# Sliding dilated attention with a gated FFN on one core: V kept twice in lines of positions, and a tile's eight copies of V loaded in two pieces

## The chip, the cores and the metric

The kernel runs on one core of one Trainium2 chip. The metric is the device time of one execution in microseconds; the time before is 239.39 us, the median of three runs (238.27 to 239.54). Names of engines in the profile: PE is TensorE's matmuls and PEld its weight loads, DVE is VectorE, ACT is ScalarE, POOL is GpSimd and SP is SyncE.

## The reference

A transformer block on 2048 positions of width 512, in bf16. Six vectors of modulation come from a small matrix product with a conditioning vector. The attention has 32 heads of 16 columns; each position looks at itself and at seven earlier positions, two apart.

```python
h = _layernorm(x) * (1 + ca) + sa
qkv = h @ wqkv                          # 32 heads of 16
idx = pos[:, None] - 2 * arange(8)      # the eight positions looked at
logits = einsum('bhsd,bhswd->bhsw', q, k[idx]) * scale    # -1e9 where idx < 0
attn = softmax(logits)
o = einsum('bhsw,bhswd->bhsd', attn, v[idx])
x = x + ga * (o @ wo)
h = _layernorm(x) * (1 + cb) + sb
x = x + gb * ((silu(h @ w1) * (h @ w3)) @ w2)             # inner width 1792
```

## The kernel before

**Tiles.** The 2048 positions are 16 tiles of 128. The first normalization and the projections of Q, K and V go by five groups of tiles: 0 and 1, 2 and 3, 4 to 7, 8 to 11, 12 to 15 (`LN1`). The normalized rows of a group are turned by TensorE (`tr`, groups 0 to 2) or by DMA transposes (groups 3 and 4, that is tiles 8 to 15); ScalarE or VectorE scales the turned rows with the modulation (L621, L644, L651), and TensorE makes Q, K (L691) and V (L711) of them. The attention goes by pairs of tiles, the FFN by six groups.

**Logits.** Q and K lie with the columns of the heads on the partitions, so that one VectorE multiplication per tile (L742, 128 x 4096) makes the products of all eight offsets: K is just read 2 w positions further back. TensorE sums over the 16 columns of a head, 32 positions at a time in four parts of the array (L752). VectorE takes maximum, difference, sum and reciprocal, ScalarE the exponential, and VectorE scales a pair's weights (L797, one operation for both tiles).

**Values.** For V the positions must be shifted across partitions. So ScalarE copies a tile of V from the PSUM into one of three buffers (L721), a DMA stores it in an HBM scratch with one row per position, after 16 rows of zeros, and four loads bring a tile's eight shifted copies back (`values`): each load takes 32 positions, as 16 pairs of rows by eight offsets, in runs of two rows (2 KB). A tile's copies go to one of three buffers: two of their own (`vsh`) and one on top of the QKV weights (`vshx`), free once these have been used for the last time. VectorE multiplies the copies by the weights in place (L827, 128 x 4096), TensorE sums them over the offsets with 0/1 matrices (L855, eight matmuls), ScalarE evicts (L861), a DMA transpose turns the result, TensorE multiplies by wo (L867), and VectorE adds to x (L871).

**What sets the order.** The whole order is written out: `ORDER` is a list of operation numbers, from which each engine, and SyncE's queue of DMAs, takes its own in turn, and `SLOTS` gives each value its PSUM bank or buffer. `synchronize` puts in the waits: for what an operation reads, and for all users of what its buffer held before. A load of V waits for the store of its tile and of the tile before. Nearly every DMA is issued by SyncE (one line, L124), in one queue; a wait at its head holds up everything behind it. The late weight loads (w1, w3 and w2 in four groups each, wo, the second modulation) have places of their own among them.

Of the kernel before, what the change touches and what calls it, by code (L numbers as in the profile page):

```python
# [10 lines left out]
P = 128  # L11
# [4 lines left out]
W = 8  # L16
# [5 lines left out]
PAD = 16  # L22
EPS = 1e-5
# [50 lines left out]
class Program:  # L74
# [41 lines left out]
    def dma(self, out, in_, key, packets, r=(), w=(), part=(), after=(), eng="sp", cost=450, group=None, transpose=False,  # L116
# [11 lines left out]
        ns = 600 if transpose else each * (126 if again else packet_ns(size))  # L128
# [140 lines left out]
AC_OLD = ()  # L269
# [3 lines left out]
def _build(p, A_x, A_wqkv, A_wo, B_w1, B_w3, B_w2, c, w_mod, out):  # L273
# [34 lines left out]
    ind = sb([P, 16], bf, "ind")  # L308
    ind2 = sb([P, 2, 32], bf, "ind2")
    before = sb([P, W, 2, 16], bf, "before")  # L310
# [29 lines left out]
    v_dram = nc.dram_tensor("v_scratch_dram", (PAD + S, D), bf)  # L340
# [20 lines left out]
    def held(pool, items):  # L361

        vals = []
        for i, item in enumerate(items):
# [7 lines left out]
    vind2 = Val("ind2")  # L372
# [16 lines left out]
                                           pattern=[[-W, 16]], channel_multiplier=1), 200, k, w=[vind])  # L389
    p.op("pool", lambda e: e.affine_select(out=ind[:], in_=ind[:], compare_op=ALU.is_ge, fill=0.0, base=W - 1,  # L390
                                           pattern=[[W, 16]], channel_multiplier=-1), 200, k, w=[vind])
    p.op("dve", lambda e: e.memset(ind2[:], 0.0), 80, k, w=[vind2])
    for y in range(2):
        p.op("dve", lambda e, y=y: e.tensor_copy(bass.AP(ind2, 33 * y, [[64, P], [2, 16]]), ind[:]), 150, k, r=[vind], w=[vind2])
    p.op("pool", lambda e: e.memset(before[:], 0.0), 250, k, w=[vbefore])
    p.op("pool", lambda e: e.affine_select(out=before[:], in_=before[:], compare_op=ALU.is_ge, fill=BEFORE, base=0,
                                           pattern=[[-DIL, W], [1, 2], [2, 16]], channel_multiplier=0), 400, k, w=[vbefore])
# [46 lines left out]
    p.dma(v_dram[0:PAD, :], zrow[:], ("load", 11), (16, 1024), r=[vzrow] + wm_hold, w=[vvpad], store=True)  # L444
# [260 lines left out]
    def proj_v(T, tt, vh):  # L705
        k = ("v", T)
        vp = Val("ps_v", psum)

        def mm(e, ts):
            for t in ts:  # L710
                ins = e.matmul(bank(vp), vh.at[:, t, tt * P:(tt + 1) * P], wqkv[:, t, 2 * D:3 * D], start=(t == ORDER[0]),  # L711
                               stop=(t == ORDER[-1]))
            return ins

        proj(mm, MM, k, vh, vp, [vwv[0], vwv[0], vwv[1], vwv[1]])
        vt = Val("v", vpool)

        def ev(e):
            dst = bass.AP(vt.at, 0, [[D, P], [H, DH], [1, H]])
            src = bass.AP(PALL, bank(vp).offset, [[8 * 512, P], [1, DH], [DH, H]])  # L720
            return e.activation(dst, src, ACT.Copy)  # L721
# [9 lines left out]
    def logits(Ts):  # L731

        vl = Val("ps_l", psum)
        for i, T in enumerate(Ts):
# [11 lines left out]
            def red(e, i=i, T=T, vp=vp):  # L746
                c0 = vl.at * 512 + i * W * 32
                if T == 0:
                    e.matmul(PALL[0:32, c0:c0 + W * 32], ones[:, 0:32], before[:], start=True, stop=False, tile_position=(0, 0))
                for ft in range(KT):  # L750
                    for q in range(4):
                        ins = e.matmul(PALL[32 * q:32 * q + 32, c0:c0 + W * 32], E_sb[:, ft, :], bass.AP(vp.at, ft * P + 32 * q, [[W * KT * P, P], [KT * P, W], [1, 2], [2, 16]]),  # L752
# [36 lines left out]
    def softmax(Ts, vl, ve, vx_):  # L789
# [7 lines left out]
        p.op("dve", lambda e: e.tensor_tensor(ve.at[0][:, 0:n], bass.AP(PALL, bank(vl).offset, [[8 * 512, P], [W * 32, n], [1, 32], [32, W]]),  # L797
                                              bass.AP(ve.at[2], 0, [[64, P], [32, n], [1, 32], [0, W]]), ALU.mult),
             74 + 267 * n, k, r=[vr, vx_], w=[va], hold=[ve, vl], lead=o, lock=False)
        vt, val = Val("ps_at", psum), Val("al", alpool)  # L800

        def turn(e):
            b = bank(vt).bitcast(bf)
            for i in range(n):
                at = b[:, i * 256:(i + 1) * 256].rearrange("p (q y h) -> p q y h", q=4, y=2)
                for y in range(2):
                    ins = e.transpose(at[:, :, y, :], bass.AP(ve.at[0], i * W * 32 + y * 16 * W, [[2 * W * 32, P], [1, P]]), ident[:])
            return ins
# [6 lines left out]
    def values(T, i, val):  # L815
# [17 lines left out]
        if T in AC_OLD:  # L833
            def acc(e):
                b = bank(vo)
                for g in range(8):
                    for ft in range(KT):
                        ins = e.matmul(b[:, ft * P + 16 * g:ft * P + 16 * g + 16], vv.at[:, g, ft * P:(ft + 1) * P], ind[:],
                                       start=True, stop=True)
                return ins  # L840

            p.op("pe", acc, C_ACC, ("ac", T), r=[vv, vind], w=[vo])
    
            def ev(e):
                dst = bass.AP(vt.at, 0, [[KT * P, P], [32, 4 * KT], [1, 2], [2, 16]])
                src = bass.AP(PALL, bank(vo).offset, [[8 * 512, P], [32, 4 * KT], [16, 2], [1, 16]])
                return e.activation(dst, src, ACT.Copy)

            p.op("act", ev, c_act(512), ("ac", T), r=[vo], w=[vt])
        else:  # L850
            def acc2(e):
                c0 = vo.at * 512
                for y in range(2):
                    for q in range(4):
                        ins = e.matmul(PALL[32 * q:32 * q + 32, c0:c0 + 512], ind2[:, y, :], vv.at[:, 2 * q + y, :], start=(y == 0),  # L855
                                       stop=(y == 1), tile_position=(0, 32 * q))
                return ins

            p.op("pe", acc2, C_RED, ("ac", T), r=[vv, vind2], w=[vo], tiled=True)
            va = Val("ac", acpool)  # L860
            p.op("act", lambda e: e.activation(va.at[:], bank(vo), ACT.Copy), c_act(512), ("ac", T), r=[vo], w=[va])  # L861
            p.dma(lambda: vt.at[:], lambda: va.at[:], ("ot", T), (128, 1024), r=[va], w=[vt], cost=1270, transpose=True)
# [75 lines left out]
    for gi, Ts in enumerate(LN1):  # L938
# [4 lines left out]
        for i, T in enumerate(Ts):  # L943
            proj_v(T, i, vh)
# [132 lines left out]
```

## Time and profile before

| | us |
|---|---|
| median of the runs | 239.39 |
| profiled execution, first to last instruction | 237.7 |
| PE busy | 229.7 |
| DVE busy | 179.4 |
| ACT busy | 138.5 |
| DMA engines, mean rate | 163 GB/s |

The span of the profiled execution is 1.7 us below the median of the runs; what lies around the first and last instruction is not in it. A row of a timeline gives the start in us, the time in us, the engine, the line, the operation, what it writes and reads, the number of operations put together, and in brackets the idle time of the engine ahead of it with what ended it. A row of windows gives, for each stretch, the stretch's length and the busy time of each engine, then the clock granted to TensorE, the busy share of the 16 DMA engines, and the GB/s that they moved. A row of groups gives count, busy time, mean ns of one, and idle time ahead.

The DMAs of V in the profile: 64 loads of 256 KB (a median of 5.5 us from issue to landing in `vsh`, 4.6 in `vshx`), and 16 stores of 128 KB (6.4 us).

### The profile page before, as it was taken

What the parts mean: (1) busy time and instruction counts of PE and PEld (TensorE: products, weight loads), DVE (VectorE), ACT (ScalarE), POOL (GpSimd) and SP (SyncE); (2) the same over time, 40 slices, a digit from 0 to 9 for tenths busy, and PEclk for the clock granted to TensorE, in tenths of its full rate; (3) what the DMA queues carried; (4) which work ended last, traced back from release to release, by engine and by line L of the source; (5) the groups of instructions that cost most, each with busy time, mean ns of one, the idle gap of its engine ahead of it and who ended that gap; (6) DMA issues with size and microseconds to landing.
All of it is one profiled execution on the core that took longest, in us unless ns stands there. A gap on an engine that the chain in (4) does not pass through costs nothing.

```text
span 237.7 us, 4535 instructions
## 1 busy us (share of the span) xinstructions
PE 229.7 (97%) x1781; PEld 136.2 (57%) x1806; DVE 179.4 (75%) x279; ACT 138.5 (58%) x267; POOL 29.2 (12%) x66
## 2 busy tenths in 40 slices
PE   7999999999999998999999999999999999999995
PEld 4776454445588674664444444444475457485774
DVE  5699999999999989999999999682654403434433
ACT  2289577999978744985865594837473405040300
POOL 4434100013002000240002520012010000000000
PEclk9999999999999999999999999999999999999999
DMA  6999999999999999897981693642203000000202
GB/s 216 372 337 322 158 237 299 208 269 283 353 200 270 243 249 199 173 260 177 247 234 47 182 234 72 154 132 46 67 19 91 3 0 0 6 19 0 70 0 88
DMA packets 46317, 38.85 MB, mean 163 GB/s; under 512 B 21704, under 2 KB 37080, under 8 KB 46296
## 3 DMA queue, kind: packets, MB, share of 16 engines
q1 hardware_dynamic: 46288, 38.56, 66.9%
q8 instruction: 14, 0.23, 0.4%
q14 instruction: 7, 0.06, 0.1%
q10 hardware_dynamic: 8, 0.00, 0.0%
HBM read 29.62 MB, written 4.21 MB: 142 GB/s over the span
## 4 chain that ended last, share of the span: by engine, by line
PE 74%; DMA 8%; DVE 8%; SPq 4%; ACT 3%; issue 2%; ACTq 0%; DVEq 0%
PE pall L883 38%; PE pall L921 18%; DMA sb_x<-in_A_x_dram 5%; PE pall L867 5%; SPq L124 4%; PE pall L691 4%; DMA sb_vsh<-v_scratch_dram 3%; PE pall L909 3%; PE pall L855 2%; PE pall L752 2%; PE pall L711 2%; DVE sb_vsh L827 2%; DVE sb_pq L742 2%; DVE sb_hh L892 1%; ACT sb_h L621 1%
## 5 line engine op out<-in xcount | busy, mean ns | idle before, releaser
L883 PE MATMUL pall<-sb_h,sb_w 128*128 128x256 bf16 (+1 forms) x664 | 101.9, 307 | 1.8 <-DVE sb_hh L892 0.9
L883 PEld LDWEIGHTS pall<-sb_h,sb_w 128*128 128x128 bf16 x672 | 64.8, 98 | 37.2 <-issue 2.8
L889 ACT ACTIVATE sb_sg<-pall 128x256 bf16<-128x256 f32 (+1 forms) x84 | 35.6, 453 | 54.1 <-PE pall L883 53.0
L892 DVE TENSOR_TENSOR sb_hh<-sb_sg,pall 128x256 bf16<-128x256 bf16 (+1 forms) x84 | 39.9, 505 | 34.8 <-PE pall L883 32.7
L921 PE MATMUL pall<-sb_w,sb_hh 128*128 128x512 bf16 x190 | 44.0, 379 | 0.3
L742 DVE TENSOR_TENSOR sb_pq<-sb_q,sb_kT 128x4096 bf16<-128x4096 bf16 x16 | 36.3, 2282 | 0.0
L921 PEld LDWEIGHTS pall<-sb_w,sb_hh 128*128 128x128 bf16 x196 | 19.0, 98 | 21.6 <-DVE sb_hh L892 0.4
L691 PE MATMUL pall<-sb_h,sb_wqkv 128*128 128x512 bf16 (+1 forms) x154 | 30.2, 335 | 0.5 <-issue 0.2
L827 DVE TENSOR_TENSOR sb_vsh<-sb_vsh,sb_al 128x4096 bf16<-128x4096 bf16 x12 | 27.3, 2287 | 2.1 <-DMA sb_vsh<-v_scratch_dram 2.1
L621 ACT ACTIVATE sb_h<-sb_h,sb_modc 128x512 bf16<-128x512 bf16 (+1 forms) x24 | 16.5, 743 | 10.1 <-DMA sb_h<-sb_xn 10.1
L691 PEld LDWEIGHTS pall<-sb_h,sb_wqkv 128*128 128x128 bf16 x160 | 14.7, 98 | 11.8 <-ACT sb_ac L861 0.4
L931 DVE TENSOR_TENSOR sb_o<-pall,sb_x 128x512 bf16<-128x512 f32 (+1 forms) x18 | 11.1, 625 | 10.5 <-PE pall L921 6.8
L711 PE MATMUL pall<-sb_wqkv,sb_h 128*128 128x512 bf16 x62 | 15.5, 379 | 0.2
L867 PE MATMUL pall<-sb_wo,sb_ot 128*128 128x512 bf16 x61 | 15.3, 379 | 0.3 <-issue 0.2
L586 POOL TENSOR_SCALAR sb_nm<-sb_sx 128x2 f32<-128x2 f32 x8 | 1.7, 218 | 105.2 <-DVE sb_x L871 105.1
L644 ACT ACTIVATE sb_h<-pall,sb_modc 128x256 bf16<-128x256 bf16 (+1 forms) x18 | 9.9, 612 | 7.5 <-DVE sb_modc L509 6.5
L861 ACT ACTIVATE sb_ac<-pall 128x512 bf16<-128x512 f32 x16 | 9.5, 595 | 7.2 <-PE pall L855 7.1
L601 ACT ACTIVATE sb_xn<-sb_x,sb_nb,sb_rs 128x512 bf16<-128x512 bf16 x16 | 12.4, 806 | 0.7 <-POOL sb_nb L599 0.6
L871 DVE SCALAR_TENSOR_TENSOR sb_x<-pall,sb_x 128x512 bf16<-128x512 f32 x16 | 10.9, 686 | 1.5 <-PE pall L867 1.3
L590 ACT ACTIVATE sb_xn<-sb_x,sb_nm 128x512 bf16<-128x512 bf16 x16 | 11.4, 714 | 0.7 <-POOL sb_nm L586 0.7
L721 ACT ACTIVATE sb_v<-pall 128x512 bf16<-128x512 f32 x16 | 9.5, 600 | 2.8 <-PE pall L711 2.8
L555 DVE BATCH_NORM_STATS2 sb_st<-sb_x 128x6 f32<-128x512 bf16 x16 | 10.6, 680 | 0.8 <-DMA sb_x<-in_A_x_dram 0.7
(87 smaller groups left out, 208.3 us busy)
## 6 DMA issues: line engine op xcount, KB each, us to landing
sb_vsh<-v_scratch_dram SPq DMA_DIRECT2D x48, 256.0 KB, 5.5
sb_vshx<-v_scratch_dram SPq DMA_DIRECT2D x16, 256.0 KB, 4.6
sb_w<-in_B_w_dram SPq DMA_DIRECT2D x6, 512.0 KB, 7.9
sb_w<-in_B_w_dram SPq DMA_DIRECT2D x6, 384.0 KB, 5.4
v_scratch_dram<-sb_v SPq DMA_DIRECT2D x16, 128.0 KB, 6.4
out_dram<-sb_o SPq DMA_DIRECT2D x14, 128.0 KB, 1.8
sb_wqkv<-in_A_wqkv_dram SPq DMA_DIRECT2D x6, 256.0 KB, 6.3
sb_x<-in_A_x_dram SPq DMA_DIRECT2D x4, 256.0 KB, 6.4
```

The costliest lines, as they stand in the source:

```text
L590: p.op("act", lambda e, vn=vn, T=T: e.activation(vn.at[:], x_sb[:, T, :], ACT.Square, bias=nm[:, T, :], accum_out=var[:, T, :]), c_act(512 ...
L601: p.op("act", lambda e, vn=vn, T=T: e.activation(vn.at[:], x_sb[:, T, :], ACT.Identity, bias=nb[:, T, :], scale=rs[:, NT + T, :]), c_act(5 ...
L621: return e.activation(vh.at[:, ft, 0:n * P], vh.at[:, ft, 0:n * P], ACT.Identity, bias=modc[:, 8 * which + ft:8 * which + ft + 1], scale=m ...
L691: ins = e.matmul(bank(vp)[:, j * n:(j + 1) * n], wqkv[:, t, col:col + P], vh.at[:, t, 0:n], start=(t == ORDER[0] and j == 0), stop=(t == O ...
L711: ins = e.matmul(bank(vp), vh.at[:, t, tt * P:(tt + 1) * P], wqkv[:, t, 2 * D:3 * D], start=(t == ORDER[0]), stop=(t == ORDER[-1]))
L742: return e.tensor_tensor(vp.at[:], in0, in1, ALU.mult)
L827: return e.tensor_tensor(v_w, v_w, a_w, ALU.mult)
L867: ins = e.matmul(bank(vy), vt.at[:, ft, :], wo[:, ft, :], start=(ft == 0), stop=(ft == KT - 1))
L883: ins = e.matmul(bank(vp)[:, 0:n], wt[:, t, fi * P:(fi + 1) * P], vh.at[:, t, 0:n], start=(t == 0), stop=(t == KT - 1))
L889: p.op("act", lambda e: e.activation(vt.at[:, 0:n], bank(vgp)[:, 0:n], ACT.Silu), c_act(n), k, r=[vgp], w=[vt], table="silu")
L892: p.op("dve", lambda e: e.tensor_tensor(vh_.at[:, 0:n], vt.at[:, 0:n], bank(vup)[:, 0:n], ALU.mult), c_dve(n), k, r=[vt, vup], w=[vh_])
L921: ins = e.matmul(bank(vz), vhh[fi].at[:, tt * P:(tt + 1) * P], w2[:, fi, :], start=(fi == 0), stop=(fi == NF - 1))
```

## The change

The scratch becomes 64 lines of 66 x 512 + 256 elements, 68,096 bytes each. Position p stands in line 32 + p mod 32 at column p div 32 (copy 0), and a second time in line p mod 32 at column p div 32 + 1 (copy 1); a column is one position's 512 elements, and 16 rows of zeros stand in lines 16 to 31 at column 0. So the positions 32 a + i - d of four neighbouring a, for any d up to 14, stand side by side in line 32 + i - d.

- A tile's copies come in two loads of 512 KB, each with 32 lines by four offsets in runs of four columns (4 KB): one load has the offsets 0, 4, 8, 12, the other 2, 6, 10, 14.
- A tile's V is stored by two DMAs of 128 KB, one for each copy. For the stores to be even, a matmul of V takes every n-th position of its group of n tiles instead of 128 neighbours, so the weights that TensorE loads stand n elements apart (n is 2 or 4), and the loads of every tile of a group wait for all stores of that group and of the group before.
- The sums over heads, the scaling of the softmax (two operations for a pair instead of one), the transposes of the weights and the sums over offsets take the new order of offsets; one 0/1 matrix (`ind`) does for all of the eight sums, and `ind2` and an operation on `before` go.
- `ORDER`: the operations of TensorE, VectorE, ScalarE and GpSimd keep their order, but for those that are gone. SyncE's list is a new one. `SLOTS` is new too: 223 of 326 PSUM banks are others, and some of the buffers of V, of its copies and of the results.

```diff
-        vd = Val("vd")
-        p.dma(v_dram[PAD + T * P:PAD + (T + 1) * P, :], lambda: vt.at[:], k, (128, 1024), r=[vt], w=[vd], cost=400, store=True)
-        vv_dram[T] = vd
+        for copy in range(2):
+            p.dma(bass.AP(v_dram, (32 * (1 - copy) + b) * VL + (4 * Ts[0] + copy) * D, [[D, 4 * n], [n * VL, 32 // n], [1, D]]), lambda: vt.at[:], k,
+                  (128, 1024), r=[vt], part=[vv_dram[T]], cost=400, store=True)
...
-                ins = e.matmul(bank(vp), vh.at[:, t, tt * P:(tt + 1) * P], wqkv[:, t, 2 * D:3 * D], start=(t == ORDER[0]),
+                ins = e.matmul(bank(vp), bass.AP(vh.at, 512 * t + b, [[KT * 512, P], [n, P]]), wqkv[:, t, 2 * D:3 * D], start=(t == ORDER[0]),
...
-        for q in range(4):
-            p.dma(lambda q=q: vv.at[:, 2 * q:2 * q + 2, :],
-                  bass.AP(v_dram, (PAD + T * P + 32 * q) * D, [[2 * D, 16], [-DIL * D, W], [1, 2 * D]]), ("vl", T), (128, 2048),
+        for y in range(2):
+            p.dma(lambda y=y: vv.at[:, 4 * y:4 * y + 4, :],
+                  bass.AP(v_dram, (32 - DIL * y) * VL + 4 * T * D, [[VL, 32], [-2 * DIL * VL, 4], [1, 4 * D]]), ("vl", T), (128, 4096),
...
+        def scale(e):
+            for i in range(n):
+                ins = e.tensor_tensor(bass.AP(ve.at[0], i * W * 32, [[2 * W * 32, P], [P, 2], [4, 32], [1, 4]]),
+                                      bass.AP(PALL, bank(vl).offset + i * W * 32, [[8 * 512, P], [P, 2], [1, 32], [32, 4]]),
+                                      bass.AP(ve.at[2], 32 * i, [[64, P], [0, 2], [1, 32], [0, 4]]), ALU.mult)
...
-                        ins = e.matmul(PALL[32 * q:32 * q + 32, c0:c0 + 512], ind2[:, y, :], vv.at[:, 2 * q + y, :], start=(y == 0),
+                    ins = e.matmul(PALL[32 * q:32 * q + 32, c0:c0 + 512], ind[:], vv.at[:, 4 * y + q, :], start=(y == 0),
```

SyncE's list around the places where it differs most, in words: up to the store of the zero rows it is as before. Then, before: the stores of tiles 0 and 1, half of the second modulation, the store of tile 2, the four transposes of tiles 8 to 11, the eight loads of tiles 0 and 1. Now: the second group of w3 (512 KB, before among the loads of about 55 us), half of the second modulation, the six stores of tiles 0, 1 and 2, the four transposes, the four loads of tiles 0 and 1 with a store of tile 3 among them. Later the first group of w1 comes behind the transposes of tiles 12 to 15 instead of ahead of three of them, and the fourth group of w1 behind the stores of tile 7 (before at 43 us).

More of the change, by code (lines that the diff above doesn't have):

```diff
@@ L127, in dma @@
         each = -(-n // 16)
-        ns = 600 if transpose else each * (126 if again else packet_ns(size))
+        ns = 600 if transpose else each * (160 if again else packet_ns(size))
         o = self.op(eng, fn, cost, key, r=r, w=w, part=part, after=after, dma=(each, ns, *(lat if lat else (900, 200) if store else (900, 500) if transpose else (1300, 600))))
@@ L307, in _build @@
     ones = sb([P, 256], bf, "ones")
-    ind = sb([P, 16], bf, "ind")
-    ind2 = sb([P, 2, 32], bf, "ind2")
-    before = sb([P, W, 2, 16], bf, "before")
+    ind = sb([P, 32], bf, "ind")
+    before = sb([P, 48], bf, "before")
     cst = sb([P, 2], f32, "cst")
@@ L338, in _build @@
     vsh_x = nc.alloc_sbuf_tensor_at("sb_vshx", [P, 8, D], bf, offset=nc.lookup_mloc(wqkv).addr)
[L340 removed]
+    v_dram = nc.dram_tensor("v_scratch_dram", (64, VL), bf)
     PALL = ctx.enter_context(nc.psum_tensor("pall", [P, 8 * 512], f32))
@@ L388, in _build @@
     p.op("pool", lambda e: e.affine_select(out=ind[:], in_=ind[:], compare_op=ALU.is_ge, fill=0.0, base=0,
[L389 to L394, printed above, removed]
+                                           pattern=[[-4, 32]], channel_multiplier=1), 200, k, w=[vind])
+    p.op("pool", lambda e: e.affine_select(out=ind[:], in_=ind[:], compare_op=ALU.is_ge, fill=0.0, base=3,
+                                           pattern=[[4, 32]], channel_multiplier=-1), 200, k, w=[vind])
     p.op("pool", lambda e: e.memset(before[:], 0.0), 250, k, w=[vbefore])
-    p.op("pool", lambda e: e.affine_select(out=before[:], in_=before[:], compare_op=ALU.is_ge, fill=BEFORE, base=0,
-                                           pattern=[[-DIL, W], [1, 2], [2, 16]], channel_multiplier=0), 400, k, w=[vbefore])
+    p.op("pool", lambda e: e.memset(before[:, 0:14], BEFORE), 80, k, w=[vbefore])
     vstep = Val("step")
@@ L443, in _build @@
               bass.AP(A_wo.tensor, A_wo.offset + dl * D, [[16 * D, H], [4 * D, KT], [1, D]]), ("load", 10), (128, 1024), part=[vwo])
-    p.dma(v_dram[0:PAD, :], zrow[:], ("load", 11), (16, 1024), r=[vzrow] + wm_hold, w=[vvpad], store=True)
+    p.dma(bass.AP(v_dram, 16 * VL, [[VL, PAD], [1, D]]), zrow[:], ("load", 11), (16, 1024), r=[vzrow] + wm_hold, w=[vvpad], store=True)
     for name, a, i in (("wms1", 0, 12), ("wms1b", 512, 26)):
@@ L832, in values, with acc2 @@
         vt = Val("ot", otpool)
[L833 to L862, printed above, removed]
+        def acc2(e):
+            c0 = vo.at * 512
+            for y in range(2):
+                for q in range(4):
+                    ins = e.matmul(PALL[32 * q:32 * q + 32, c0:c0 + 512], ind[:], vv.at[:, 4 * y + q, :], start=(y == 0),
+                                   stop=(y == 1), tile_position=(0, 32 * q))
+            return ins
+        p.op("pe", acc2, C_RED, ("ac", T), r=[vv, vind], w=[vo], tiled=True)
+        va = Val("ac", acpool)
+        p.op("act", lambda e: e.activation(va.at[:], bank(vo), ACT.Copy), c_act(512), ("ac", T), r=[vo], w=[va])
+        p.dma(lambda: vt.at[:], lambda: va.at[:], ("ot", T), (128, 1024), r=[va], w=[vt], cost=1270, transpose=True)
         vy = Val("ps_y", psum)
@@ L942, in _build @@
         proj_qk(gi, Ts, 1, vh)
-        for i, T in enumerate(Ts):
-            proj_v(T, i, vh)
+        vd = Val("vd")
+        for T in Ts:
+            vv_dram[T] = vd
+        for b in range(len(Ts)):
+            proj_v(Ts, b, vh)
     gate(0)
```

18 lines of the change are left out of this document (8 added, 10 removed), and 131 rows, old and new, of tables (ORDER, SLOTS).

## The prediction

> **What bounds the kernel now.** I read the page first, then the windows by stage, then the timelines of the queue, ScalarE, TensorE and VectorE around the V loads.
>
> ```profile
> span 237.7 us, 4535 instructions
> ...
> PE 229.7 (97%) x1781; PEld 136.2 (57%) x1806; DVE 179.4 (75%) x279; ACT 138.5 (58%) x267; POOL 29.2 (12%) x66
> ...
> DMA  6999999999999999897981693642203000000202
> ```
> ```profile
> core 0: us, PE busy (x) PEld busy (x) DVE busy (x) ACT busy (x) POOL busy (x), PEclk, DMA share, GB/s
> 14.00:18.00 4.00, 4.00 (x49) 3.13 (x48) 4.00 (x11) 3.38 (x8) 1.91 (x4) 1.00 1.11 326
> 18.00:24.00 6.00, 5.95 (x63) 3.92 (x61) 5.91 (x17) 5.78 (x11) 2.66 (x6) 1.00 1.10 326
> 24.00:28.00 4.00, 3.88 (x49) 1.82 (x47) 4.00 (x4) 1.61 (x4) 0.00 (x0) 1.00 1.80 109
> 28.00:38.00 10.00, 9.89 (x83) 5.25 (x82) 9.96 (x15) 8.61 (x16) 0.89 (x2) 1.00 1.06 238
> 66.00:90.00 24.00, 23.03 (x225) 17.40 (x226) 22.32 (x34) 16.05 (x35) 1.31 (x4) 1.00 1.14 242
> ```
>
> TensorE is busy 229.7 of 237.7 us and its order is fixed, so the end moves by what is added to or taken out of its gaps: 8.0 us in all. VectorE is as full: 9.96 of 10 us in 28 to 38, 22.32 of 24 in 66 to 90. The DMA line stands at 9 from its second to its sixteenth slice of 5.94 us: up to about 95 us the DMA engines are a third full resource, and transfers land in the order in which SyncE issues them. So the change is read from where a transfer lands late for one of the full engines. That happens at two V loads:
>
> ```profile
> 60.31 2.29 DVE L827 TENSOR_TENSOR sb_vsh<-sb_vsh,sb_al 128x4096 bf16<-128x4096 bf16 x1 [0.26 <-DMA sb_vsh<-v_scratch_dram]
> ...
> 87.14 2.29 DVE L827 TENSOR_TENSOR sb_vsh<-sb_vsh,sb_al 128x4096 bf16<-128x4096 bf16 x1 [1.04 <-DMA sb_vsh<-v_scratch_dram]
> ...
> 158.73 2.29 DVE L827 TENSOR_TENSOR sb_vsh<-sb_vsh,sb_al 128x4096 bf16<-128x4096 bf16 x1 [0.85 <-DMA sb_vsh<-v_scratch_dram]
> ```
> ```profile
> 89.82 1.05 PE L883 MATMUL pall<-sb_h,sb_w 128*128 128x256 bf16 x8 [0.87 <-DVE sb_hh L892]
> ...
> 93.19 0.61 PE L855 MATMUL pall<-sb_vsh,sb_ind 128*32 128x512 bf16 x8 [0.36 <-DVE sb_vsh L827]
> ```
>
> VectorE stands still for 0.26 us (tile 2) and 1.04 us (tile 7), and TensorE's longest gap, 0.87, follows from the second. The third wait, 0.85 at 158.73, is followed by no gap of TensorE in this list; I count it at nothing.
>
> **The change, part by part.** First the traffic. A tile's V loads stay at 1 MB, but in 4 KB runs instead of 2 KB. Before, a stretch of almost nothing but these loads (28 to 38) moved 238 GB/s, so a tile takes 4.4 us of the queue. No row has 4 KB runs: the bounds are 238 GB/s (4.4 us, no gain) and the 326 of the weight loads in 14 to 24 (3.2 us). I take 3.2, since 1 KB runs that are each read once already reach it. Each tile's second store adds 128 KB, 0.4 us at 326. Per tile the queue gains 0.8 us, between -1.2+0.4 and +0.4.
>
> SyncE issues 32 loads fewer and 16 stores more. An issue is some 0.6 us in the queue's timeline, but SyncE waits elsewhere in the same stretches; I count this at nothing.
>
> The gain: the waits of 0.26 and 1.04 go if tile 7's loads land 1.04 earlier. In the new list the 512 KB load of w3's second group (1.6 us at 326) leaves the stretch ahead of them, and tiles 4 to 7 save 0.8 each: together 4.8, more than is needed. Next late at 87 is VectorE itself, which has no other wait there. Gain: 1.3 us. The 0.36 at 93.19 stays, as VectorE and TensorE both move.
>
> The loss is where that weight load goes: ahead of everything that follows the zero row, with six stores (tiles 0, 1, 2, both copies) where there were three, and all that ahead of the DMA transposes of tiles 8 to 11.
>
> ```profile
> 14.73 2.59 SPq L124 DMA_DIRECT2D v_scratch_dram<-sb_zrow  x1
> 17.36 0.91 SPq L124 DMA_DIRECT2D v_scratch_dram<-sb_v  x2
> 18.31 0.46 SPq L124 DMA_DIRECT2D sb_wm_s<-in_w_mod_dram  x1
> 18.82 1.39 SPq L124 DMA_DIRECT2D v_scratch_dram<-sb_v  x1
> 21.03 5.66 SPq L124 DMA_TRANSPOSE sb_h<-sb_xn  x4
> 26.80 1.06 SPq L124 DMA_DIRECT2D sb_vsh<-v_scratch_dram  x1
> ```
> ```profile
> L124 SPq DMA_TRANSPOSE sb_h<-sb_xn x4: 1267/1288/1684, 21.0 to 25.4; - x4
> ...
> DMA to landing us min/median/max: 4.6/5.8/7.5
> ```
> ```profile
> 26.74 0.60 ACT L721 ACTIVATE sb_v<-pall 128x512 bf16<-128x512 f32 x1 [2.39 <-PE pall L711]
> ...
> 27.71 0.60 ACT L721 ACTIVATE sb_v<-pall 128x512 bf16<-128x512 f32 x1
> ...
> 30.61 2.96 ACT L621 ACTIVATE sb_h<-sb_h,sb_modc 128x512 bf16<-128x512 bf16 x4
> ```
> ```profile
> 33.33 1.89 PE L691 MATMUL pall<-sb_h,sb_wqkv 128*128 128x512 bf16 x7
> ```
>
> The last of the four transposes is issued at 25.4 and lands no sooner than 4.6 later, at 30.0. ScalarE scales them at 30.61 without having waited: 0.6 us of cover. The four operations end at 33.57, and TensorE's Q matmuls of these tiles start in the group of 33.33, after four of an earlier group: no further cover. Ahead of the transposes the new list has 512 KB (weights) and 3 x 128 KB (stores) more: 0.92 MB, at 326 GB/s 2.8 us. So ScalarE starts them 2.8 - 0.6 = 2.2 us later, and so does TensorE.
>
> A second path leads to the same place. With the new buffer numbers, tile 4's V eviction (26.74) still takes tile 0's buffer, and now waits for two stores of tile 0, behind two 512 KB loads and with a store of tile 2 between them; tile 3's takes tile 2's buffer instead of tile 1's, and tile 5's that of tile 1, whose stores come last. Tile 0's store landed after this:
>
> ```profile
> L124 SPq DMA_DIRECT2D v_scratch_dram<-sb_v x3: 431/432/1386, 17.4 to 18.8; - x3
> ...
> DMA to landing us min/median/max: 7.0/7.5/9.5
> ```
>
> 17.4 + 7.0 = 24.4 at the soonest. Add 1 MB of loads (3.2) and two stores (0.8): 28.4, that is 1.7 after 26.74. Queued behind this eviction on ScalarE are the evictions up to the scaling at 30.61, and TensorE waits for their banks. This delay runs beside the 2.2 and is smaller, so it adds nothing. Bounds of the early loss: none, if the added bytes find room (first rival), and 5.2 (second rival).
>
> On VectorE one scaling of a pair becomes two:
>
> ```profile
> L892 DVE TENSOR_TENSOR sb_hh<-sb_sg,pall 128x256 bf16<-128x256 bf16 x56 | 21.8, 417 | 25.2 <-PE pall L883 24.9
> ...
> L797 DVE TENSOR_TENSOR sb_attn<-pall,sb_ssum 128x512 bf16<-128x512 f32 x8 | 5.5, 688 | 0.2
> ```
>
> Apart, 2 x 417 - 688 = 0.15 us per pair; from 28 to 100 us, where VectorE is full, there are five pairs: some 0.4 with the overlap of neighbours. The removed constants of VectorE and GpSimd lie ahead of the first normalization, and TensorE runs warm-up matmuls there: nothing.
>
> TensorE's V matmuls now load weights whose columns are 2 or 4 elements apart, and the logits' sums read runs of 32 instead of every second element.
>
> ```profile
> L711 PEld LDWEIGHTS pall<-sb_wqkv,sb_h 128*128 128x128 bf16 x64 | 6.1, 98 | 6.6 <-ACT sb_v L721 0.4 <-ACT sb_q L700 0.2
> ```
> ```profile
> 29.94 1.89 PE L711 MATMUL pall<-sb_wqkv,sb_h 128*128 128x512 bf16 x8
> ...
> 45.97 1.06 PE L752 MATMUL pall<-sb_pq,sb_E 128*32 128x256 bf16 x32
> ```
>
> Eight V matmuls take 1.89, one each 0.216 with the last one's tail of 0.38; a weight load of 98 ns hides in that up to 2.2 times its length. The sums with every second element, four at a time, already run at 1.06 for 32, the pace of their columns. So zero for both, as that row is the nearest; were a spaced load four times 98 ns, 64 x (0.39 - 0.216) = 11 us would be the other end. [...]
>
> The sum, against the profiled execution: 237.7 + 2.2 - 1.3 + 0.4 = 239.0, or 1.3 more. The median of the runs is 239.39, 1.7 above the span; with that around it: **240.7 us**. About 0.5%, 1.2 us, is what a measurement of this kernel can tell from no change.
>
> **The rivals.** *The hole takes it in (not slower).* From 24 to 28 the engines moved 109 GB/s instead of 326: 0.87 MB of room, as much as is added. If the transposes were held up there by something other than the queue, the stores and the weights fill the hole, and the transposes land within their cover. Then 237.7 - 1.3 + 0.4 = 236.8, or 238.5 with what lies around, and 238.1 if the second scaling of a pair hides too. For it: the size of the hole. Against: the hole lies behind the transposes' first issue and the plain transfers ahead of them, so it looks like their own slowness, which comes later too. It decides at more than 2.2 us of hidden delay.
>
> *Half the engines.* A pair's store (tiles 0 to 3) has 8 outermost lines of columns; if its packets go to 8 of 16 engines, each of the six stores takes 0.8 us there instead of 0.4: 2.4 more, or 5.2 - 0.6 = 4.6 early and 243.1 in all.
>
> ```profile
> q10 hardware_dynamic: 8, 0.00, 0.0%
> ...
> sb_c<-in_c_dram ACTq DMA_DIRECT2D x1, 1.0 KB
> ```
>
> For it: the only short-sided transfer of the trace, four rows of c, has eight packets on its own queue, four for the data and four to report, where a 16-engine transfer would have 16 to report. [...] Against: the other eight engines carry none of these stores and reach the transposes early, so the loss is full only if a transpose waits for its slowest engine.
>
> *4 KB runs bring nothing.* At 238 GB/s the queue pays 0.4 per tile for the second stores. Over tiles 0 to 7 that is 3.2, less the 1.6 of the moved load; the waits at 60 and 87 stay, and the early 2.2 with them: 237.7 + 2.2 + 0.4 + 0 to 1.6, some 242 with what lies around. Against: the same bytes in 1 KB runs reach 326.
>
> **How the numbers follow.** The forecast has 0.38 (239.8 to 241.6: the early loss between 1.3 and 3.1), of it 0.17 within 0.5% and 0.21 slower; the hole 0.36, of it 0.20 faster and 0.16 within, as 238.1 lies on the border of 238.2; half the engines 0.18, all slower; no gain from 4 KB runs 0.08, of it 0.01 within and 0.07 slower. That gives 0.20 faster, 0.34 the same, 0.46 slower. The range reaches from 237.8, below the hole's 238.1, to 243.2, just above half the engines; some 0.18 lies outside.
>
> **What would show it.** Right: the four transposes of tiles 8 to 11 land at about 32.8 and L621 has a wait for them; L721's eviction at 26.7 waits for a DMA; TensorE's first Q matmuls of tiles 8 to 11 come 2 us later; the waits of L827 for loads at 60 and 87 are gone, and 512 KB loads of V land some 1.6 us apart. Wrong: ScalarE scales those tiles at 30.6 as before (the hole), TensorE loses over 4 us before 40 (half the engines), or L827 waits as long as before (4 KB runs); a PE busy time above 231 would point at the spaced weight loads.

## The result and the profile after

The changed kernel takes 247.21 us (median of four runs, 245.81 to 247.88) beside 239.15 us for the kernel before: a ratio of 1.033, with a 95% interval of 1.029 to 1.037. By the ratio that is 7.9 us more, as it is by the spans of the two profiled executions (245.6 against 237.7); the median lies 4.0 us above the top of the predicted range, 243.2. Medians further down are of all executions of a kernel, while ratios leave out those more than 1.5% above its fastest: five of eleven in e6, at most one in any other changed kernel.

Line numbers have moved: L621 of before is L615 now, L711 and L721 (V) are L706 and L716, L867 is L849, L883 is L865; L827 stays. The page after, the rows that answer to those of before:

```profile
span 245.6 us, 4559 instructions
...
PE 232.8 (95%) x1806; PEld 136.4 (56%) x1806; DVE 180.4 (73%) x284; ACT 138.5 (56%) x267; POOL 32.1 (13%) x66
...
DMA  6999999699599977597560397570522100000102
```

TensorE's busy time looks 3.1 us longer, but that is the recording: 25 matmuls are missing from the trace of before (1781 against 1806). Three later runs that keep the old layout and whose traces hold all 1806 (e4, e9, e14) show 232.2 to 233.1 us busy, as much as the changed kernel's 232.8. So nearly all of the 7.9 us are gaps, and the 8.0 us of gaps that the prediction counted were nearer to 5, as an estimate from these three. The windows of the changed kernel show where the new gaps lie:

```profile
24.00:28.00 4.00, 4.00 (x56) 2.01 (x52) 4.00 (x4) 0.51 (x1) 0.00 (x0) 1.00 1.46 251
28.00:38.00 10.00, 8.89 (x78) 4.68 (x75) 8.96 (x16) 8.70 (x16) 0.88 (x2) 1.00 0.94 241
48.00:54.00 6.00, 5.10 (x48) 2.25 (x36) 5.93 (x12) 3.67 (x7) 0.22 (x1) 1.00 0.80 218
54.00:60.00 6.00, 5.50 (x29) 2.68 (x30) 5.63 (x7) 5.28 (x12) 3.48 (x2) 1.00 1.00 321
60.00:66.00 6.00, 2.48 (x17) 1.22 (x16) 4.86 (x4) 2.85 (x6) 3.04 (x2) 1.00 0.68 250
66.00:90.00 24.00, 23.70 (x236) 16.44 (x234) 19.70 (x33) 20.73 (x43) 1.30 (x4) 1.00 0.95 283
```

Before, the three stretches of 48 to 66, which the prediction does not show, had been full:

```profile
48.00:54.00 6.00, 6.00 (x31) 2.68 (x30) 5.73 (x13) 5.66 (x13) 1.31 (x4) 1.00 0.98 284
54.00:60.00 6.00, 5.95 (x44) 2.98 (x46) 6.00 (x4) 5.91 (x13) 1.64 (x1) 1.00 1.07 283
60.00:66.00 6.00, 5.77 (x79) 3.87 (x72) 5.71 (x6) 5.89 (x13) 0.00 (x0) 1.00 1.19 329
```

The second number is TensorE's busy time: 1.0 us less than before in 28 to 38, then 0.9, 0.5 and 3.5 us short in 48 to 66, and 0.7 more than before in 66 to 90. TensorE's timeline of the changed kernel names the gaps, in brackets:

```profile
35.67 1.04 PE L685 MATMUL pall<-sb_h,sb_wqkv 128*128 128x512 bf16 x4 [0.86 <-ACT sb_h L615]
...
54.50 2.76 PE L685 MATMUL pall<-sb_h,sb_wqkv 128*128 128x512 bf16 x12 [1.40 <-ACT sb_v L716]
64.02 0.29 PE L630 MATMUL pall<-sb_ident,sb_xn 128*128 128x128 bf16 x2 [3.01 <-ACT sb_xn L595]
64.82 0.49 PE L630 MATMUL pall<-sb_ident,sb_xn 128*128 128x128 bf16 x6 [0.51 <-ACT sb_xn L595]
...
103.07 1.04 PE L849 MATMUL pall<-sb_wo,sb_ot 128*128 128x512 bf16 x4 [1.03 <-DMA sb_ot<-sb_ac]
```

The first was predicted, though as 2.2 us. The last is a transpose of the attention that landed late. Several runs below have such a wait near 100 too (0.58 to 1.25 us: e1, e4, e5, e7, e8, e9, e15), under the old list and the new, and what brings it was not tried. The chain of work that ended last tells the story of the three between. Its columns are start, duration, and what it was:

```profile
49.36 4.47 DMA v_scratch_dram<-sb_v
54.93 1.43 ACT sb_xn L584 x4
56.44 1.54 POOL sb_rs L590
58.05 2.71 POOL sb_rs L591
60.83 2.30 POOL sb_nb L593
63.18 0.69 issue
63.87 0.81 ACT sb_xn L595
65.31 0.93 PE pall L685 x4
```

ScalarE's waits in the changed kernel (total us, times, longest) say who waited for a store:

```profile
ACT sb_h L615 <- DMA sb_h<-sb_xn: 10.7, 3, 3.9
ACT sb_v L716 <- DMA v_scratch_dram<-sb_v: 7.1, 4, 4.1
...
ACT sb_xn L595 <- POOL sb_nb L593: 4.5, 2, 3.9
```

The trace of before has no such wait at the V eviction (L721 there, L716 now). Now ScalarE stands still four times, 7.1 us in all, because a V buffer is not free until both stores of its last tile have landed. The longest, 4.06 us ahead of tile 4's eviction at 28.57, takes the place of a wait of 2.39 for TensorE; the one that matters is tile 9's, 2.33 us until 53.85. SyncE's timeline, changed kernel:

```profile
48.08 0.59 SPq L125 DMA_DIRECT2D v_scratch_dram<-sb_v  x1
48.71 0.59 SPq L125 DMA_DIRECT2D sb_w<-in_B_w_dram  x1
49.36 1.89 SPq L125 DMA_DIRECT2D v_scratch_dram<-sb_v  x3
```

The first row is tile 6's first store, the second a 512 KB load of w1, the third begins with tile 6's second store. It lands behind the load, at 53.8, and only then does ScalarE evict tile 9 into that buffer. Behind this eviction stand the softmax and the squares of the second normalization of tiles 0 and 1 (L584), and behind those three tiny GpSimd steps. These go wrong for a reason of their own, as the timelines of GpSimd and VectorE side by side suggest:

```profile
56.44 1.53 POOL L590 TENSOR_SCALAR sb_rs<-sb_var 128x2 f32<-128x2 f32 x1 [3.51 <-ACT sb_xn L584]
58.05 2.70 POOL L591 TENSOR_TENSOR sb_rs<-sb_rs,sb_cst 128x2 f32<-128x2 f32 x1
60.83 2.29 POOL L593 TENSOR_TENSOR sb_nb<-sb_nm,sb_rs 128x2 f32<-128x2 f32 x1
```
```profile
55.64 2.28 DVE L737 TENSOR_TENSOR sb_pq<-sb_q,sb_kT 128x4096 bf16<-128x4096 bf16 x1
...
57.91 2.28 DVE L737 TENSOR_TENSOR sb_pq<-sb_q,sb_kT 128x4096 bf16<-128x4096 bf16 x1
60.77 2.29 DVE L827 TENSOR_TENSOR sb_vsh<-sb_vsh,sb_al 128x4096 bf16<-128x4096 bf16 x1 [0.58 <-DMA sb_vsh<-v_scratch_dram]
```

Each GpSimd step works on 128 x 2 numbers, and each ends after the VectorE multiplication beside which it started: 57.97 after 57.92, 60.75 after 60.19, 63.12 after 63.06. In the trace of before the same three took 0.19, 0.71 and 1.82 us. There, and in e1 and e7, only the third starts beside such a multiplication, and it ends 0.04 to 0.06 us after it. So in these rows a step that starts beside a long multiplication ends 0.04 to 0.56 us behind it; by what mechanism is not shown. The other way round nothing shows, as a multiplication that started at 53.31 beside the second step of before took its usual 2.28 us.

### The profile page after: what moved, and what is told of

It reads as the page before. It is cut to its first block, busy times and chain, and to the rows that moved or that the text cites. A ratio compares the mean times of both kernels' runs of the same rounds, so it can differ in the third digit from the quotient of the medians.

```text
span 245.6 us, 4559 instructions
## 1 busy us (share of the span) xinstructions
PE 232.8 (95%) x1806; PEld 136.4 (56%) x1806; DVE 180.4 (73%) x284; ACT 138.5 (56%) x267; POOL 32.1 (13%) x66
## 4 chain that ended last, share of the span: by engine, by line
PE 68%; DMA 12%; DVE 7%; ACT 6%; SPq 3%; POOL 3%; issue 1%; ACTq 0%
PE pall L865 37%; PE pall L903 14%; DMA sb_ot<-sb_ac 5%; PE pall L849 4%; PE pall L685 3%; DVE sb_st L549 3%; SPq L125 3%; DMA sb_x<-in_A_x_dram 3%; ACT sb_h L615 3%; PE pall L891 2%; PE pall L837 2%; DMA sb_h<-sb_xn 2%; PE pall L747 2%; DMA v_scratch_dram<-sb_v 2%; DVE sb_pq L737 2%; PE pall L706 1%
## 5 line engine op out<-in xcount | busy, mean ns | idle before, releaser
L865 PE MATMUL pall<-sb_h,sb_w 128*128 128x256 bf16 (+1 forms) x672 | 102.7, 308 | 0.2
L865 PEld LDWEIGHTS pall<-sb_h,sb_w 128*128 128x128 bf16 x672 | 64.9, 98 | 36.1 <-issue 1.7
L903 PE MATMUL pall<-sb_w,sb_hh 128*128 128x512 bf16 x196 | 44.9, 379 | 0.0
L685 PE MATMUL pall<-sb_h,sb_wqkv 128*128 128x512 bf16 (+1 forms) x160 | 31.4, 337 | 2.6 <-ACT sb_v L716 1.4
L827 DVE TENSOR_TENSOR sb_vsh<-sb_vsh,sb_al 128x4096 bf16<-128x4096 bf16 x12 | 27.4, 2290 | 3.6 <-DMA sb_vsh<-v_scratch_dram 2.2
L615 ACT ACTIVATE sb_h<-sb_h,sb_modc 128x512 bf16<-128x512 bf16 (+1 forms) x24 | 16.5, 734 | 10.8 <-DMA sb_h<-sb_xn 10.7
L849 PE MATMUL pall<-sb_wo,sb_ot 128*128 128x512 bf16 x64 | 16.0, 380 | 1.2 <-DMA sb_ot<-sb_ac 1.2
L706 PE MATMUL pall<-sb_wqkv,sb_h 128*128 128x512 bf16 x64 | 16.0, 380 | 0.0
L716 ACT ACTIVATE sb_v<-pall 128x512 bf16<-128x512 f32 x16 | 9.7, 603 | 7.5 <-DMA v_scratch_dram<-sb_v 7.1
L584 ACT ACTIVATE sb_xn<-sb_x,sb_nm 128x512 bf16<-128x512 bf16 x16 | 11.4, 714 | 1.7 <-POOL sb_nm L580 1.7
```

The source lines that it names most:

```text
L615: return e.activation(vh.at[:, ft, 0:n * P], vh.at[:, ft, 0:n * P], ACT.Identity, bias=modc[:, 8 * which + ft:8 * which + ft + 1], scale=m ...
L685: ins = e.matmul(bank(vp)[:, j * n:(j + 1) * n], wqkv[:, t, col:col + P], vh.at[:, t, 0:n], start=(t == ORDER[0] and j == 0), stop=(t == O ...
L706: ins = e.matmul(bank(vp), bass.AP(vh.at, 512 * t + b, [[KT * 512, P], [n, P]]), wqkv[:, t, 2 * D:3 * D], start=(t == ORDER[0]), stop=(t = ...
L827: return e.tensor_tensor(v_w, v_w, a_w, ALU.mult)
L849: ins = e.matmul(bank(vy), vt.at[:, ft, :], wo[:, ft, :], start=(ft == 0), stop=(ft == KT - 1))
L865: ins = e.matmul(bank(vp)[:, 0:n], wt[:, t, fi * P:(fi + 1) * P], vh.at[:, t, 0:n], start=(t == 0), stop=(t == KT - 1))
```

## The experiments

Three theories were set against each other. **A**: the V buffers' release, with the chain above. **B**: SyncE's new list as a whole, with the buffer slots that came with it. **C**: the layout itself (doubled stores, spaced weights). Two came later, for what is left under the old list: **S**, SyncE's serial issue of the extra stores, and **T**, their bytes.

| run | what differs | median us | ratio to the kernel before | 95% interval |
|---|---|---|---|---|
| after | | 247.21 | 1.033 | 1.029 to 1.037 |
| e1 | after, 8 V buffers | 242.77 | 1.016 | 1.008 to 1.024 |
| e7 | after, one store ahead of one load | 244.07 | 1.020 | 1.015 to 1.025 |
| e8 | after, early w3 load put back | 246.56 | 1.029 | 1.023 to 1.035 |
| e4 | before, with the new list and slots | 242.47 | 1.015 | 1.009 to 1.021 |
| e2 | new layout, old list and slots | 241.56 | 1.011 | 1.004 to 1.018 |
| e5 | e2, 8 V buffers | 243.38 | 1.019 | 1.012 to 1.026 |
| e6 | e2, w1 load behind two transposes | 242.22 | 1.008 | 1.004 to 1.012 |
| e13 | e6, 8 V buffers | 241.60 | 1.009 | 1.005 to 1.013 |
| e9 | before, second store to nowhere | 244.97 | 1.026 | 1.021 to 1.032 |
| e12 | e9, 8 V buffers | 245.45 | 1.026 | 1.021 to 1.032 |
| e14 | e9, stores of 16 KB | 242.27 | 1.014 | 1.010 to 1.017 |
| e15 | e9, ScalarE issues the second store | 243.04 | 1.016 | 1.014 to 1.019 |
| e10 | e6, ScalarE issues the second store | 240.88 | 1.007 | 1.003 to 1.010 |
| e11 | e6, GpSimd issues the second store | 241.87 | 1.014 | 1.007 to 1.021 |
| e16 | e10, 8 V buffers | 242.43 | 1.011 | 1.007 to 1.015 |

**Eight V buffers in the changed kernel (e1).**

```diff
-    vb = [sb([P, D], bf, f"v{i}") for i in range(3)]
+    vb = [sb([P, D], bf, f"v{i}") for i in range(8)]
```
(`SLOTS` deals the eight in the order of the evictions.)

> The changed kernel with eight V buffers instead of three (one more line of slots, all orders kept). Theory A, the chain from the V buffers (ScalarE's V eviction waits for both stores of the buffer's last tile, ScalarE is late for LayerNorm 2 of tiles 0 and 1, GpSimd's small steps fall among VectorE's long ones): the wait of 7.1 us at the V eviction goes, and with it the TensorE gaps of 1.40 at 54.5 and of 3.01 and 0.51 at 64, some 4.9 us: 242.3 us, and 241 to 244. Theory B, the new list of SyncE (big weight loads ahead of stores, V loads and transposes): the wait goes but the gaps stay or move, 245.5 to 247.5. Theory C, the layout itself (twice the stored bytes, weight loads with a spacing): nothing moves, 246.5 to 247.5.

242.77 us, as A had it: 4.4 us come back by the medians, 4.1 by the ratios. ScalarE no longer waits at its V eviction, the gaps at 54 and 64 are gone, and GpSimd's three steps take 0.19, 0.70 and 1.90 us. TensorE's waits in e1 (total, times, longest) are for late transfers, and for steps that waited for one:

```profile
PE pall L849 <- DMA sb_ot<-sb_ac: 1.6, 2, 0.9
...
PE pall L837 <- DVE sb_vsh L827: 1.0, 3, 0.6
PE pall L685 <- ACT sb_h L615: 0.7, 1, 0.7
```

**One exchange in the list (e7).**

```diff
 SyncE: store V tile 6, copy 0
+SyncE: store V tile 6, copy 1
 SyncE: load w1, first group (512 KB)
-SyncE: store V tile 6, copy 1
```

> The changed kernel with one exchange in SyncE's list: the second store of tile 6's V is issued ahead of the 512 KB load of w1 that stood before it. Theory A (the chain: that store held ScalarE's eviction of tile 9 until 53.8, ScalarE was late for LayerNorm 2 of tiles 0 and 1, and GpSimd's three steps then fell one after the other under VectorE's long multiplications): the store lands 3 us earlier, the gaps of 1.40, 3.01 and 0.51 all shrink, 242.5 to 244. Rival A2 (the 3 us at 64 come from the V loads and VectorE alone, whatever ScalarE does): only the 1.40 goes, 245.4 to 246.2. Theory B: 246 to 247.5.

244.07 us: one exchange gives back 3.1 us. The store lands at 51.4 instead of 53.8, GpSimd's first step comes 2.3 us earlier, and only the third is long. GpSimd's timeline in e7:

```profile
54.15 0.19 POOL L590 TENSOR_SCALAR sb_rs<-sb_var 128x2 f32<-128x2 f32 x1 [1.66 <-ACT sb_xn L584]
54.42 0.70 POOL L591 TENSOR_TENSOR sb_rs<-sb_rs,sb_cst 128x2 f32<-128x2 f32 x1
55.21 1.87 POOL L593 TENSOR_TENSOR sb_nb<-sb_nm,sb_rs 128x2 f32<-128x2 f32 x1
```

The gaps of 3.01 and 0.51 are gone; another of 1.43, for a V eviction, stands at 64.2. The time is just above A's range and well below A2's. So A's chain from the store to the stall is shown, and A2, by which only 1.40 would have gone, falls. GpSimd's part in it was not tried by itself; it is read from the time stamps.

**The early weight load put back (e8).**

```diff
-SyncE, behind the zero row: load w3, second group (512 KB)
 SyncE: load w3, first group (512 KB)
+SyncE: load w3, second group (512 KB)
```

> The changed kernel with the load of w3's second group (512 KB), which the new list issues at 17 us, put back to about its old place at 60 us. The prediction's first term: the transposes of tiles 8 to 11 land 1.5 us earlier (31 instead of 32.7), and the 0.86 us gap at 35.7 goes; the extra stores' half speed remains, so not the whole 2.2. If the later stalls stay as they are: 246.0 to 246.6. If the later stalls hang on this delay too: 243 to 245. If the load now arrives late for the FFN: 247 to 249.

246.56 us, 0.65 less (1.0 by the ratios), which is within the intervals. The last transpose of tiles 8 to 11 lands at 31.5 instead of 32.7 (30.1 before), and the gap of 0.86 is gone. The later stalls stay. So the early load, the larger part of the prediction's 2.2 us, is worth about a microsecond at most, and the runs do not tell it from nothing.

**Layout and list apart (e2, e4).** In e2 each store became two at its old place and each tile's loads took the places of the second and fourth of its old four; in e4 the kernel before got the new list, its one store standing at the place of the second copy.

> The new layout with the list and the buffer slots of the kernel before: each V store is two at its old place, each tile's two loads stand at the places of the second and fourth of its old four. Theory A: three V buffers are still each released by two stores, so about half of the loss stays, 243 to 245. Theory B: the loss goes nearly whole, 239 to 241. Theory C: 246 to 248.

> The kernel before (one store, four loads of 2 KB runs) with the new list and slots: the store of a tile at the place of its second copy, the four loads as two neighbours at each place. Theory A: a buffer is released by one store, though at the later place, so some of the chain stays, 242 to 245. Theory B: the list's loss is there without the layout, 244.5 to 247.5. Theory C: 239 to 240.5.

Counted from 239 us, the layout alone costs 2.6 us (1.011), between A's and B's range, and the list with its slots 3.6 (1.015), within A's; together they cost 7.9. Both parts are to blame, and neither A, B nor C alone. The 1.7 us that come only from both are less than the three intervals leave open. In e4 the V eviction waits too, with one store per tile (ScalarE's waits in e4):

```profile
ACT sb_v L721 <- DMA v_scratch_dram<-sb_v: 6.5, 4, 3.1
```

So the list and its slots make the buffers scarce, with bulky loads ahead of stores; that the second store makes it worse fits the 7.9, but is not shown by itself. The list and the slots were not tried apart: they also deal the V buffers anew, so that tile 9 takes tile 6's buffer in e4 and in the changed kernel, and tile 10's before and in e2. In e2 there is no such wait, and TensorE waits for over 0.3 us past 28 us only twice, for transposes of the attention: 0.57 at 121, and this one for its first tile, queued behind a load of w1 (TensorE's timeline in e2):

```profile
50.55 2.17 PE L849 MATMUL pall<-sb_wo,sb_ot 128*128 128x512 bf16 x8 [1.36 <-DMA sb_ot<-sb_ac]
```

**What is left under the old list (e5, e6, e13).** e6 issues that load behind the two transposes; e5 and e13 have eight buffers, without and with this move. (The load is of 384 KB; the expectation says 512.)

```diff
-SyncE: load w1, last group
 SyncE: transpose attention tile 0
 SyncE: store V tile 10, copies 0 and 1
 SyncE: transpose attention tile 1
+SyncE: load w1, last group
```

> The new layout with the list of the kernel before (three V buffers), and one 512 KB load of w1 moved behind the transposes of attention tiles 0 and 1 on SyncE. In the run without this move TensorE waited 1.36 us at 49.2 for the first of these transposes, which landed 0.46 us behind that load. Theory B (what is left with the old list is SyncE's queue: the extra stores make it issue the transposes 2 us later, and the load ahead of them is the last of it): the wait goes and the time falls by 1.0 to 1.5, to 239.8 to 240.6. Theory C (the layout costs elsewhere, the wait only shows it): another wait takes its place, 241.2 to 241.8.

> The new layout with the list of the kernel before and eight V buffers. Theory A: no V buffer is waited for, 239.5 to 241.5. Theory B: the same as with the old list and three buffers, 239 to 241. Theory C: 246 to 248. Against the run with the old list and three buffers: under A it is 2 us or more faster, under B within 1 us.

> The new layout with the old list, the w1 load behind the first two attention transposes, and eight V buffers. Theory A: buffers still hold back ScalarE in some executions, so this one is the faster of the two and steadier, 239 to 240.5. Theory S: the buffers are not waited for under this list, so as with three, 240 to 242. The kernel before is at 239.6 in this comparison if nothing is left of the loss.

In e6's profile the wait at 50 is gone, one of 0.40 is left at 119, and the span is 238.1; but that is the fastest of its eleven executions. Its median, 242.22, is above what B and C gave it, and its ratio is 1.008: the move gives at most some tenths of a per cent, within the intervals. Buffers give nothing here, 1.009 in e13, as S had it (e13 is the steadier of the two, nine of its ten executions within 240.8 to 243.5, but not the faster): A holds under the new list only. e5 came out at 1.019, above what A and B gave it; its interval overlaps that of e2, its profile has a stall of 2.0 us for the same transposes, and why it is not nearer to e2 stays open.

**What a second store costs by itself (e9, e12, e14, e15).** The kernel before, in its old layout and list, stores each tile of V once more to lines that nothing reads. The other three change the number of buffers, the size or the issuer.

```diff
         vv_dram[T] = vd
+        p.dma(v_dup[T * P:(T + 1) * P, :], lambda: vt.at[:], k, (128, 1024), r=[vt], cost=400, store=True)
```

> The kernel before, its old layout, loads and list, with one store more for each V tile: the same buffer written once more to lines that nothing reads. It has the doubled stores without the 4 KB loads. Theory A/B (doubled stores cost SyncE 0.6 us of issue each and hold the V buffers longer, and the fewer loads pay it back): slower than the new layout under the same list, 242 to 244. Theory C (the stores are hidden, the rest of the layout costs): 239 to 240.

> The kernel before with the second store of each V tile to lines that nothing reads, and eight V buffers instead of three. With three buffers it took 5.4 us more than the kernel before. Theory A (the second store costs by holding the V buffer): 239.5 to 241.5. Theory S (it costs SyncE's issue time, and transposes and loads behind it come late): 243.5 to 245.5.

> The kernel before with one store more for each V tile to lines that nothing reads, of 16 of its 128 rows (16 KB instead of 128 KB), issued by SyncE. With the whole rows it took 5.4 us more than the kernel before. Theory S (SyncE's issue, 0.6 us for each): 243.5 to 245.5, no matter how few the bytes. Theory T (bytes on the shared engines): 239.5 to 241.

> The kernel before with the second store of all 128 rows to lines that nothing reads, issued by ScalarE one step after its eviction. Theory S: SyncE has its old work, 239.5 to 241.5. Theory T: 243.5 to 245.5, as with SyncE issuing them.

Sixteen stores of 128 KB cost 6.3 us by the ratio (2.6% of 239.6) and 5.4 by the medians, so theory C falls. Buffers are not it (e12). With an eighth of the bytes 3.3 us remain, between what S and T gave it. The bytes can hardly explain them; the issue is the likeliest: SyncE's entry takes 0.43 us in the trace (16 times, 420 to 1227 ns), and what stands behind it is late. With SyncE freed, 3.8 us remain, of which bytes and ScalarE's own 0.33 us per issue were not told apart. So S is about half of it, and T at most the other half. TensorE's waits in e9:

```profile
PE pall L869 <- DMA sb_ot<-sb_ac: 3.0, 4, 1.2
PE pall L885 <- DVE sb_hh L894: 1.7, 1, 1.7
```

These are transposes of the attention, late in SyncE's queue, and an FFN step behind a V load. The new layout under the same list (e2) costs 2.6 us. That its larger loads, fewer and faster, give back the other 3.7 of the 6.3 is a difference of two ratios and was not tried: the two kernels differ in other things too, such as the shape of the stores and loads that wait for a whole group's stores.

**Other issuers (e10, e11, e16).** The second copy's store gets another queue, ScalarE's or GpSimd's, on top of e6; e16 adds eight buffers.

```diff
-                  (128, 1024), r=[vt], part=[vv_dram[T]], cost=400, store=True)
+                  (128, 1024), r=[vt], part=[vv_dram[T]], cost=400, store=True, eng="act" if copy else "sp")
```

> The new layout with the old list and the w1 load behind the first two attention transposes, and the second store of each V tile issued by ScalarE, one ScalarE step after its eviction, instead of SyncE. SyncE then issues 16 DMAs fewer. Theory S (the stores cost SyncE's serial issue, 0.6 us each): the transposes of the first attention tiles land a microsecond or two earlier than in the run with the old list and nothing else, no wait for them is left, 238.5 to 240. Theory T (the stores cost their bytes on the shared engines and the V buffers): as that run with the moved load, 240 to 242. If ScalarE pays for the issue as SyncE did, 16 times 0.6 of which a part lies on the path: 241 to 244.

> The same with GpSimd issuing the second stores, at the places that they had in the list. Theory S: 238.5 to 240, as GpSimd is idle for most of the time to 50 us. Theory T: 240 to 242. If GpSimd's work for a DMA waits behind VectorE's long steps as its small steps did at 56 to 63 us of the changed kernel: the stores of the first tiles go out late, V loads wait for them, 242 to 248.

> The new layout with the old list, the w1 load behind the first two attention transposes, ScalarE issuing the second stores, and eight V buffers. Theory S with buffers of no weight under this list: as with three buffers, 240 to 241.5, no gain on the kernel before. If the V loads' freed SyncE time and the vanished waits of VectorE for them (2.1 us in the kernel before) reach the end: 237.5 to 239.

e10 is the best of the new layout at 1.007 (240.9 us, in T's range and above S's); its profiled execution, the fastest of twelve, has a span of 237.6, as the kernel before. Against e6's 1.008 this is no difference: taking sixteen issues off SyncE gives back nothing that stands clear of the noise here. e11 and e16 came out higher, with intervals that overlap e10's, and e16 above what S gave it. None beats the kernel before.

## Why the prediction was wrong

**The step that failed** is the one on the V buffers: "This delay runs beside the 2.2 and is smaller, so it adds nothing." It was worked out for tile 4's eviction alone, and there it held: the eviction waited until 28.57 (28.4 in the prediction), and TensorE lost 0.25 us. But the same rule, two stores to land before a buffer is free, holds for all 13 evictions that reuse a buffer, and the list was not read on for which store stands behind which load. Tile 9's eviction, behind tile 6's second store, cost gaps of 4.9 us with all that follows it; eight buffers give back 4.4 us (e1), one exchange 3.1 (e7). No rival had this mechanism. The rest, some 3.5 to 4 us, has no single cause that the runs show.

**SyncE's issue, counted at nothing**, was probably the second wrong step: in the kernel before, 16 extra entries cost 3.3 us with hardly any bytes in them (e14). In the new layout the cost is not shown: 32 loads fall away, and taking the 16 entries off SyncE changed nothing clear of the noise (e10 against e6).

**The early loss** had the right mechanism and the wrong size. The transposes landed at 32.66 (predicted 32.8), L615 waited for them until 32.69, and the Q matmuls came at 35.67 with a gap of 0.86. Putting the load back gave 0.65, of the 1.6 that the prediction counted for it. Those matmuls came 1.7 us later than before (33.98 in its trace), but of that 0.25 was tile 4's eviction and 0.5 had been lost between 6 and 12 us (5.20 us busy, before 5.69), where executions differ by themselves (5.98 in e1, with the same list). I had counted 0.6 us of cover for ScalarE, and none for the 0.4 us that TensorE still worked after ScalarE's last scaling.

**Half the engines** fits what the trace of the changed kernel shows, but is not shown itself, as no trace names the engine that carried a packet. Each store of tiles 0 to 3 has nine updates of its semaphore there, one 1.0 to 1.4 us after its issue began and eight as it lands; the load of c has five, and every other DMA 16. The first six such stores land 0.63 to 0.71 us apart, three later ones with 16 updates 0.38 and 0.32 (41.65 to 42.35). No run shows the price of 2.4 us that this rival counted. With the same six stores under the old list the last transpose lands at 30.22 (e5), 31.76 (e6) and 32.37 (e2, whose queue ran 1.0 us later from the zero row on), against 30.07 before. With the early w3 load and one store per tile, in its old shape, it lands at 30.40 (e4). So **the hole took in** the load alone, as the first rival had it, and the stores in one run of three; load and stores together did not fit, at 32.66. Why the executions differ stays open.

**4 KB runs** do better than the 326 GB/s that I assumed: back to back, between 82 and 90 us, a 512 KB V load lands 1.22 to 1.26 us after the one ahead, some 420 GB/s. From 78 to 84 us, where they make up much of the traffic, the engines move 393 GB/s against 245 before:

```profile
78.00:84.00 6.00, 6.00 (x54) 4.84 (x52) 5.41 (x13) 5.72 (x13) 0.81 (x3) 1.00 1.07 393
```

**The gain at 87** came: VectorE takes its V loads there without a wait, TensorE's 0.87 is gone, and 66 to 90 holds 0.7 us more work than before. **The gain at 60** did not: where VectorE had waited 0.26 us for a load, it now waits 0.58 at 60.77 and 0.56 at 63.63, inside the stall, and its total for V loads is 2.2 (2.1 before).

**The second scaling** of a pair costs 0.07 us (0.75 for both against 0.69), so some 0.35 for the five pairs for which the sum had 0.4.

**Spaced weights** cost the time nothing, as predicted, and because a slower load hides. TensorE's busy time is above the 231 that was to point at them, yet kernels without them show as much, as said above, and eight V matmuls in a row still take 1.89 us. The load itself is slower at 8 bytes, which the prediction's zero, an estimate from the sums over heads, did not have. These are the weight loads of V in the changed kernel, with columns 4 bytes apart (tiles 0 to 3) and 8 bytes apart (the other tiles), in ns (min/median/max):

```profile
L706 PEld LDWEIGHTS pall<-sb_wqkv,sb_h x16: 97/98/98, 11.2 to 19.6; 128*128 128x128 bf16 x16
L706 PEld LDWEIGHTS pall<-sb_wqkv,sb_h x48: 111/113/135, 25.6 to 68.6; 128*128 128x128 bf16 x48
```

Before, all had taken 98. At 8 bytes a load takes 113, which still hides behind the 0.216 us of a matmul.

## What to carry to other kernels

When a transfer is doubled or split, list for every buffer which transfer now frees it, and what stands ahead of that one in the queue; one bulky load in the wrong place cost 3 us here, and moving one entry of a list gave it back. Count entries of a busy queue as well as bytes. A late small step can meet work that it never met before, so a delay of 2.3 us became gaps of 4.9 here.

## What the runs showed of the hardware

GpSimd steps on 256 numbers took 1.53 and 2.70 us where they started beside VectorE's long multiplications (changed kernel), and 0.19 and 0.71 where they did not (before). A weight load of 128 columns that stand 8 bytes apart took 113 ns (median), 4 bytes apart or, before, side by side 98. Stores of 128 KB with nine updates of their semaphore landed 0.63 to 0.71 us apart in the changed kernel, three with 16 updates 0.38 and 0.32. SyncE spent 0.42 to 0.64 us on most plain DMAs (110 of 132 before, 93 of 116 in the changed kernel) and 1.19 to 2.62 us on a transpose. The granted clock was 0.78 in the stretch with waits of 1.50 and 0.50 us (e5, 48 to 54) but 1.00 around the stall of 3.01 in the changed kernel; why was not tried.
